# Seventeen products of zeros on TensorE, and a new order of issue on all engines

## The chip, the cores and the metric

The kernel runs on one core of a Trainium2 chip. The metric is device microseconds (us) of one execution, the median of three runs. TensorE (PE in the profile) does the matrix products, VectorE (DVE), ScalarE (ACT) and GpSimd (POOL) the rest, and SyncE (SP) issues nearly all transfers. Each engine works through its own instruction stream in order.

## The reference, cut to what matters

Attention over 4 batches of 8 heads (576 rows of 64 numbers), mixed with a memory term, feeds a gated feed-forward layer:

```python
scores = scale * np.matmul(q, k.transpose(0, 1, 3, 2))
scores = np.where(causal, -1000000000.0, scores)
a = softmax(scores)                      # a /= a.sum(-1) + 1e-09
local = np.matmul(a, v)
mem_out = einsum(phi(q), M_prev) / (einsum(phi(q), z_prev) + 1e-06)
x = g * mem_out + (1 - g) * local        # 2304 rows of 512
xn = x / rms * rms_g
out = (silu(xn @ w_gate) * (xn @ w_val)) @ w_out   # 512 -> 1536 -> 512
```

The three weight matrices arrive as 64-bit floats and are turned into 32-bit ones on the chip.

## The kernel before, in words

The 2304 rows are cut into 18 blocks of 128 rows. Blocks 0 to 3 are the first 128 rows of each batch; their attention is done in 32-bit floats, with TensorE transposes (`transposed`, L524) of k, q, phi(q) and the softmax weights S. The other blocks use pairs of 16-bit numbers. Two blocks make a chunk of 256 rows, and the feed-forward layer runs over nine chunks: `m_proj` (L1037 for chunk 0 in 32 bits, L1044 for the others) makes gate and value, `m_act` (L1061 to L1065) the activation, `m_down` (L1110, L1118 to L1120) the product with w_out.

Ahead of the first product of chunk 0 (`gv`, L1037) stand these steps, for blocks 0 and 1: `transposed` with its copies on ScalarE (L526) or VectorE (L528); the scores (`u_scores`, PE L590, then DVE L607 with the mask and the row maximum); the exponentials (`u_exp`, ACT L656, one for each of the 8 heads of a block); the transposes of S; the products with v (`pv32`, PE L790); their division (`evac32`, DVE L806) and addition to the memory term (POOL L808); the sum of squares (`x_norm`, ACT L384, then POOL L862 and L865); and `x_float`, which multiplies by a diagonal matrix (DVE L876, PE L879) and writes `xT` (DVE L880). The memory term is `mem32` (PE L767 and L771). Beside it the weights are converted: two ScalarE instructions (L955, L956) and one of VectorE (L960) for each piece of 128x512, whose transfer SyncE issues at L922. `over_partitions` (L252, L256) takes a maximum over the 128 partitions by a product with the identity; the first such product is for `zz`, the array of z_prev, whose sum of squares ScalarE makes (L384). `gram` (L272) sums products that bound the scale of k and v.

All engines' orders of issue are written out: the table `ISSUE` holds for PE, Activation, DVE, Pool and SP a string of letters, one letter for a kind of work (`T` a transpose, `s` a gram product, `Z` a maximum over partitions, `S` scores, `E` exponentials, `U` weight conversion, `G` a projection, `D` a down product, and so on), a count behind it, and `~n` to take the n-th of that kind that is left. `keep` marks the functions with their letters, and `issue_in_order` chains each engine's instructions in the table's order. Instructions still wait for their data by semaphores.

Of the kernel before, what the change touches and what calls it, by code (L numbers as in the profile page):

```python
# [62 lines left out]


ISSUE = {
    "PE": (
        "T4s4T4ZT8ZSS~1S~2S~3S4T8u4SS~1S~2S~3T4S4u4Th4T3u2~4s2T2u2~4h4sT6u3h4ush4R4s2~4ss2~3s3R4ZG2G4~6G10Zss2~3ss2~2s2T8"
        "s8T4G4G3~4G5S8ss3~3G4T4u6s2s~1sT4G4ug14g~2gT2ug16T2G2Z2G4~2Z2hs2s3~2G~2G5h3s6s3~1s4s2~2ss~1sT4s4~1ss4~4s4Tu2G3T3"
        "G5h2s4hg16u2hZ2SS~1S~2S~3g2g16~14g12Tg2S4T3u3g3G4ug13Z2G4DhD~1TZ2h2DD~1hT3G8h4D2G5D2G11D2G4G~4DG4DG11D2G12D~1D3"
        "D~1G11D~2DS2S2~6GDS12G12S2M5G6DMM6~2S8M2GM2S6G17SG12ZG12DS7G16S8G8P18GP6G12S8G33S8P9G24MP3DD~2G2M5D~2D3GP12M2S"  # L70
        "G11S~5DD3~2D5M2D3D~3DG4D~2S10G~8DG8S6M3P7D~1G2S2DP5SG9P12M3G10DD~2DD2~1DP2G2~2GPS~3S3D~3P2S2G3~1GP7DG10S3D~2DD~1"
        "DP2DD~2S4P10G4D2~2D2M3G12~5S2G8~5SMG4M~4S3M4GDD2~2D3M7G3D~3D2D2~1DD~3DS~2GS2P18S5DD~1D2P9DP9D2~2D3SG36S3G12D2S"
        "D3~1G4P2SDPG8S6P6G12M3S3PMPDD2~2D2S3~3DMS2~3S2PSP6G12P9MS~1G12P9S5~1DG12M2~2MSD2~2MG10SD3S~5GSD3S~4P3G8~1M2P2"
        "S2~4GS~4S4M2PD3G4D2~3D2G8SGG2~3M2P8GS5G9PG10P4GD~1DD~3G4S~1P3G2SPD~3D3P5G5D~1P4G5PG7PDS3P2DS4G4~5D~1S2G4S4GP7"
        "D2~1DSP2S6~1P6SG6DD~2D2G2P3DSG12P9S8~1D2~1G2SP9G10DD~1M~8G6G~6G7M9G10S3G8D~1D2G~4S~5GS~5MGS~5S5G6~2MD~3S5G2MG5D"
        "D~2P2G7MP10DGDMGSP11GS~7S5MDPGSG9~1PG4S6~1SD2D~1D2S~1PG2D~1P2SDS4G10DD3~1P17G6S~3SGP3G3G~14PDGG4~13SD2~3SGP3"
        "G6~12S2G~12G11PGP3M6D~3G3S~5P13GP3M2S4G8PDGPS8D2P10G11S2DD2~2DD~1DP12G3~12GSS3~5G5D~3G~6D~3D2MS4S~1G~6D~1DG~6S2"
        "G5~6G6D~3GP3S~3G4P7S2G3D~3PSG2~5G5MDD~2G10D~5SM2G6~12PS~6P5S6G4~12G9D2M2G2~3S6P2GG~2G2S4~1P4MGPMS3~1G7P12S~1D5S"
        "G3DD2~2D3G12P12G12S20DD~2DD~1DG21D~1GP3S20DG3~2P8G2PD2~2YP12G4M16S20P8G5D~2G3DP16G2~9G3DG6S20G11D~3D5GDD~2G4D3"
        "G18M14S20P12M2G12P18S15S~1S4P23D2D2~2G7D5D~1DPS20P36DG17P30S15S4~1SDG12D2~3D2D~1DG21SG3D2D~1G4S7G14~8SG3~8G8D3"  # L80
        "S6~7D~3DD~2DD~1S6S2~1G10SG9DG12S3DP120D2~2DD~1S2DG13M8G3~11DG6M8G4DP2S3D~1GPD3D~3D2D2~1DG42P9G4P12G10P12D2~3D4G"
        "P12G7SG5S~5D2D2~1G24S5D4D2~1SD2S4G9M2M2~6M2G3G~12G2M5~4G2M3G6S6MS6D2~3D2D~1DG11S6DD2~2DD~1DMG14S4G10S2G2D~3G2"
        "G12~10S3G6~10S6~3P12G10DD2~2SDP6G6D2~4PDS2P7G12S3DPGS2P8DS3GDG5DS8G5YG4PG6P9D5G2P2MSPGPG11S8~7DG9MP5M2S7P9GM4D~3"
        "D2D~1G2S8GS3D2SP9D3S3~4G8G12~3S~4G3D3M4S4P12G6P11G~6SG10~6DD2~2DS2S4~1G~6S2~1D~1S~1M3PSDGP8G~5G5SMG11D2D2~1DG6D"
        "G4P5G14DD~2DD2~1DG12P~11P4P4~7G12D2D2~1P7~7DP7G12DSP5G3DG9D~2DP2S4~7S7GP5S4P24D3S4G11S4D~3D2D~1MG12~12MG3SG~9G3"
        "M7~6M2S6G2~6SG11M4DG4DMD2~3D4D~3D2D2~1DP8S4S6~2P4S2G12G12~12G12S2P4D2D3~1S4P8G14P5SG6P7G5S4GSM6DG3S4MDG~7G3P12D"
        "G6~4SD~1G5~4MG7~4D2~1DG3S~1GDD~2DP6GS2D~1S3M6P2SGD~1DMG3MG12PS5P4G9S~1DGD2~2SGD~2G2~1P4GD~5D2G2PD5P9S4G26D~3S"
        "D2~3G6P5S4D2G3DP4~4S4GS3P4G5S5P2G7~3SP2G5~3G3D~3G8PD~3D2S~7P7GPGPDP3S5G2DG11DD~2P15S2G6~13GG3~12M4S3MM~3SM~3"
        "G3~12G2M3G8MD~2G~2GS~3MGS~3D3D~3S2P4S2PMG5DPD~2DD~1SDG3MG2S4G12~1G8SMD~3S~7P2MG5DD~2D2S3~7S6S2~1G2P4S3G5D~1P4G5P"
        "G12S2DD2~2DG11P7G13PS3PS3D~1DD~3DD~2D2P10G12P6~12DD3~3G12S20GP12D3G23P6D2P12M14S20G7G2~17G4M2S15S4~1SP6GD2P3"  # L90
        "G2~12D~2G9D2P3S20PG~3PDD~1P4G3P6S20D2~1G7DG12D3~3D3G24S20D~3D2D~1D2P60S16M16S4G36P30S20P30D2D3~1DG24D~3D5G23D8"
        "P120D~1G7~13G13D~1DG10D~1G7DG24DD~1D11D~1DG43D2G3DG~2G21G4~4D5G12D2G9G3~3D4G3D2D~1G7D~1D3G14DD~1D3G12G3~12G31D"
        "D~2DD~1D2G8~2G2DD~2DD~1D2G4D2D3~1G6~12DG12D5G30DG36D~3D5G8D~3D3G16D2D~3D7D3~1DD3~3D3"
    ),
    "Activation": (
        "fI~1TITfTU2TEE2~1ET2IU2E2E~1E2E2~1EE~1E~2E2NU~4UNtU3U4~3U3U~2fAtoAU2~2T3UU~8U~1U~7oU2~3AU3E2~1EfATU3TEUU2~4U2E~2"
        "U2~2EU2E~1EAU2ATxU2xU~2AU3xU2ExEE~1EU3cxNExUXU2xAEE~1EU2U2~2c2U2xU2AxU~1UNxU2XfxckAcqxAU~1Uv~1vkc3qrAxU2x2kcAFxc"
# [18 lines left out]
        "ALV3S2LA4S2LS2LS2A2V3LS2AMLAM2SASALS2LMA2MSXLSV3A2LMA2V3A2XA28O"  # L116
# [1357 lines left out]
```

## Time and profile before

| | us |
|---|---|
| median of three runs | 599.7 (598.3, 599.7, 605.78) |
| the profiled execution, its own time | 599.91 |
| its span, first to last instruction | 597.7 |
| TensorE busy | 579.4 (97%) |
| VectorE, ScalarE, GpSimd busy | 437.9, 394.8, 134.7 |

The profiled execution is 2.2 us longer than its span and 0.2 us longer than the median. The page's mean granted clock of TensorE is 0.997. A matmul's recorded duration holds its latency, so that groups in a row are read by the time from start to start, not by the mean of one.

### The profile page before, as it was taken

Reading aid. Unit: us, or ns where it says so; the run is one execution under the profiler, and the core shown is the slowest. Engines: PE = TensorE matmul, PEld = TensorE weight load, DVE = VectorE, ACT = ScalarE, POOL = GpSimd, SP = SyncE. Lnnn points to the kernel's source line nnn. Section 1 sums busy time; section 2 is a strip of 40 time slices with the busy share of each in tenths; the row PEclk is TensorE's granted clock in tenths of the full one; section 3 lists DMA queues with packets and bytes.
Section 4 is the critical chain, followed back from the end, with each engine's and each line's share of the span. In section 5 each row is a group of like instructions: output and inputs, shape, how many; then the busy total and the mean of one; then the engine's idle time right before and its main releaser. Section 6 shows DMA issues by size and latency. Waiting matters only on the chain.

```text
span 597.7 us, 15764 instructions
## 1 busy us (share of the span) xinstructions
PE 579.4 (97%) x6114; PEld 456.7 (76%) x6114; DVE 437.9 (73%) x1271; ACT 394.8 (66%) x856; POOL 134.7 (23%) x221
## 2 busy tenths in 40 slices
...
PEclk9899999999999999999999999999999999999999
...
GB/s 241 357 321 267 313 158 160 129 166 189 166 112 180 125 168 141 145 166 159 77 148 186 125 143 171 114 135 167 110 157 107 82 125 107 90 64 19 36 1 36
DMA packets 183787, 87.57 MB, mean 146 GB/s; under 512 B 165792, under 2 KB 165792, under 8 KB 183712
## 3 DMA queue, kind: packets, MB, share of 16 engines
...
q14 instruction: 27, 0.22, 0.1%
...
## 4 chain that ended last, share of the span: by engine, by line
PE 64%; DVE 15%; ACT 9%; DMA 7%; issue 3%; POOL 1%; SPq 1%; ACTq 0%; DVEq 0%
PE gv L1044 32%; PE out L1119 5%; PE out L1118 5%; PE out L1120 5%; PE sc L601 3%; DVE S L607 3%; DMA PT<-P 2%; PE gv L1037 2%; DVE P L683 2%; ACT junk L384 2%; DMA kv<-in_qkv_dram 1%; PE sc L624 1%; PE loc L714 1%; DMA wo<-in_moe_w_val_dram 1%; PE loc L715 1%
## 5 line engine op out<-in xcount | busy, mean ns | idle before, releaser
L1044 PE MATMUL gv<-xT,wgv 128*128 128x256 f16 x2304 | 295.6, 273 | 2.8 <-DVE th L1065 2.7
L1044 PEld LDWEIGHTS <-wgv 128*128 128x128 f16 x2304 | 217.0, 98 | 44.8 <-issue 5.4
L1083 POOL TENSOR_TENSOR h<-th,h 128x256 f16<-128x256 f32 x88 | 64.7, 738 | 261.8 <-ACT h L1082 238.5
L683 DVE SCALAR_TENSOR_TENSOR P<-S,P 128x512 f16<-128x512 f32 (+2 forms) x96 | 67.5, 703 | 24.2 <-ACT P L183 24.1
L1061 ACT ACTIVATE th<-gv,wt 128x256 f32<-128x256 f32 x96 | 44.9, 467 | 57.7 <-PE gv L1044 53.9
L1062 DVE SCALAR_TENSOR_TENSOR th<-th,gv 128x256 f32<-128x256 f32 x96 | 39.8, 415 | 57.0 <-ACT th L1061 56.6
L664 ACT ACTIVATE S<-S,nm 128x256 f32<-128x256 f32 (+3 forms) x112 | 69.6, 637 | 17.3 <-DVE nm L607 14.6
L183 ACT ACTIVATE P<-S 128x512 f16<-128x512 f32 (+2 forms) x96 | 57.6, 604 | 14.6 <-DMA PT<-P 13.7
L607 DVE CUSTOM_DVE_ANT_0 S<-sc,mask,qsc 128x256 f32<-128x256 f32 (+2 forms) x96 | 57.3, 610 | 11.4 <-PE sc L601 10.5
L1119 PE MATMUL out<-wo,h 128*128 128x512 f16 x176 | 63.0, 379 | 0.0
L1082 ACT CAST h<-th 128x256 f16<-128x256 f32 x88 | 34.7, 396 | 42.5 <-PE out L1120 32.2
L601 PE MATMUL sc<-kT,qT 128*128 128x128 f16 x576 | 61.0, 219 | 1.4 <-DVE nm L607 1.1
L1118 PE MATMUL out<-wo,h 128*128 128x512 f16 x176 | 62.1, 379 | 0.0
L1120 PE MATMUL out<-wo,h 128*128 128x512 f16 x176 | 61.4, 379 | 0.0
L601 PEld LDWEIGHTS <-qT 128*128 128x128 f16 x576 | 41.9, 98 | 12.2 <-issue 3.4
L1065 DVE SCALAR_TENSOR_TENSOR th<-th,wt,gv 128x256 f32<-128x256 f32 x96 | 45.8, 478 | 2.5
L1037 PE MATMUL gv<-xT,wgv 128*128 128x256 f32 x192 | 44.4, 381 | 0.6 <-DVE xT L880 0.6
L1037 PEld LDWEIGHTS gv<-xT,wgv 128*128 128x128 f32 x192 | 35.5, 190 | 6.9 <-issue 1.6
L715 PE MATMUL loc<-v,PT 128*128 128x64 f16 x288 | 39.3, 194 | 0.0
L716 PE MATMUL loc<-v,PT 128*128 128x65 f16 x288 | 39.2, 192 | 0.0
L714 PE MATMUL loc<-v,PT 128*128 128x65 f16 x288 | 39.1, 193 | 0.0
L851 POOL TENSOR_TENSOR t<-t,t 128x256 f32<-128x256 f32 x28 | 24.5, 880 | 51.8 <-DVE t L848 42.8
...
## 6 DMA issues: line engine op xcount, KB each, us to landing
...
```

The lines of the kernel that those rows point to most:

```text
L183: got = fn(*p, **k)
L601: nc.tensor.matmul(t[:, g * w + j * P : g * w + (j + 1) * P], qT[n][:, t2, h, :], kT[blk_of[(b, j)]][:, h, :], start=(t2 == 0), stop=(t2 = ...
L607: nc.vector.tensor_tensor_reduce(out=s[:, g * w : (g + 1) * w], in0=t[:, g * w : (g + 1) * w], in1=mask[:, m0 : m0 + w], scale=qsc[n][:, 5 ...
L664: nc.scalar.activation(v_, v_, AF.Exp, bias=nm[:, g : g + 1], scale=-1.0)
L683: m = nc.vector.scalar_tensor_tensor(out=p16[:, w : 2 * w], in0=s[:, :w], scalar=PSCALE, in1=p16[:, :w], op0=ALU.mult, op1=ALU.subtract)
L1037: nc.tensor.matmul(o, wgv[:, 1 + p, o0 : o0 + P], xT[0][:, cc, at], start=(cc == 0), stop=(cc == NC - 1))
L1044: nc.tensor.matmul(o, lhs, xT[c][:, rhs, :], start=(cnt == 0), stop=(cnt == 3 * NC - 1))
L1065: nc.vector.scalar_tensor_tensor(out=th, in0=th, scalar=sc_h, in1=gvp[F][:, 1, :], op0=ALU.mult, op1=ALU.mult)
L1083: nc.gpsimd.tensor_tensor(h16[:, 1], th, h16[:, 0], ALU.subtract)
L1118: nc.tensor.matmul(o, hh, whi, start=(f == 0), stop=False)
L1119: nc.tensor.matmul(o, hh, wlo, start=False, stop=False)
L1120: nc.tensor.matmul(o, hl, whi, start=False, stop=(f == NF - 1))
```

## The change

A function `fill` issues products of zeros: the weights are 128 columns of `mask`, the moving operand 256 further columns of it (both zero, 16-bit), and the result goes into a corner of a PSUM tile that the next products overwrite or do not read. The table `FILL` says how many are issued at the n-th call. `fill` is called where `over_partitions`, `total`, `gram`, `transposed`, `x_float` and `m_proj` have taken their PSUM tile; 17 are issued in all. The letter `*` places them in the PE order. All five strings of `ISSUE` are new; of their lines one of each side is shown.

```diff
+FILL = {0: 11, 1: 2, 12: 2, 14: 1, 23: 1}
 ISSUE = {
     "PE": (
-        "T4s4T4ZT8ZSS~1S~2S~3S4T8u4SS~1S~2S~3T4S4u4Th4T3u2~4s2T2u2~4h4sT6u3h4ush4R4s2~4ss2~3s3R4ZG2G4~6G10Zss2~3ss2~2s2T8"
+        "*13*~3sT4sT4s2~2T4Z2T8SS~1S~2S~3S4s3SS~1S~2S~3T8u3S4u5h4u~4sT6u3~4T2h4u3T4h4uh4s2~4ss~3s4*3R8ZG4G5~4G7ss2~3ss2~2"
...
+    fills = [0]
+
+    @keep("*")
+    def fill(t):
+        for _ in range(FILL.get(fills[0], 0)):
+            nc.tensor.matmul(t, mask[:, :P], mask[:, P : 3 * P], start=True, stop=True)
+        fills[0] += 1
+
     @keep("Z")
     def over_partitions(src, n):
         t = ps.tile([P, 512], F32, tag="sc", name="allp")
+        fill(t[:, 256:])
...
     def total(src, n):
         t = ps.tile([P, 512], F32, tag="sc", name="allp")
+        fill(t[:, 256:])
...
                     csum["kv", b, j] = ps.tile([P, 512], F32, tag="out", name=f"csum{j}")
+                    fill(csum["kv", b, j][:, 256:])
...
         t = ps.tile([P, NC, P], F32, tag="gv", name="tp")
+        fill(t[:, :2])
...
         t = ps.tile([P, NC, P], F32, tag="sc", name="xtp")
+        fill(t[:, :2])
...
             gvp[F] = ps.tile([P, 2, 2 * P], F32, tag="gv", name=f"gv{F}")
+            fill(gvp[F][:, 0])
```

The lines of the changed kernel are 13 to 17 higher than those of before: L285, L539, L605, L782, L786, L805, L895 and L1054 of it are L272, L524, L590, L767, L771, L790, L879 and L1037.

**The start of TensorE's stream.** The names are the tiles: `kv_98` k and v of block 0, `q_96` its q, `kv_103` k of block 1, `allp` the maximum over partitions, `tp` a transposed tile, `csum` a gram sum. Before:

```order
L524 MATMUL tp<-ident,kv_98 128x128 x4
L272 LDWEIGHTS kv_98
L272 MATMUL csum_621<-kv_98 128x128
...
L524 MATMUL tp<-ident,q_96 128x128 x4
L252 MATMUL allp<-ident,zq 128x128
L524 MATMUL tp<-ident,ph 128x128 x4
L524 MATMUL tp<-ident,kv_103 128x128 x4
L252 MATMUL allp<-ident,ga 128x128
```

Of the change, with 14 products of zeros, of which three rows are shown:

```order
L255 MATMUL allp<-mask 128x256
...
L255 MATMUL tp<-mask 128x256
...
L255 MATMUL csum_637<-mask 128x256
L285 LDWEIGHTS kv_98
L285 MATMUL csum_637<-kv_98 128x128
L539 MATMUL tp<-ident,kv_98 128x128 x4
...
L539 MATMUL tp<-ident,q_96 128x128 x4
...
L539 MATMUL tp<-ident,ph 128x128 x4
L264 MATMUL allp<-ident,zq 128x128
L264 MATMUL allp<-ident,ga 128x128
L539 MATMUL tp<-ident,kv_103 128x128 x4
```

Eleven products of zeros go into the tile of the first maximum, two into that of the first transpose and one into a gram sum, all ahead of the first data; the transposes of phi(q) of block 0 (`ph`) stand ahead of the product for `zq`, no longer behind it.

**ScalarE from the first copy to the last exponential of blocks 0 and 1.** Before:

```order
L526 COPY q_0_155<-tp 128x512
L506 ACTIVATE ph<-q_101 128x512
L526 COPY q_0_155<-tp 128x512
L955 ACTIVATE wgv<-wgv 128x512
L956 ACTIVATE wgv<-wgv 128x512
L526 COPY k_1_172<-tp 128x512
L656 ACTIVATE S,den<-S,nm 128x128 x4
L526 COPY q_1_179<-tp 128x512 x2
L209 ACTIVATE zhl<-zz,zs 128x32
L955 ACTIVATE wgv<-wgv 128x512
L956 ACTIVATE wgv<-wgv 128x512
L656 ACTIVATE S,den<-S,nm 128x128 x12
```

Of the change:

```order
L541 COPY q_0_168<-tp 128x512 x2
L520 ACTIVATE ph<-q_101 128x512
L212 ACTIVATE zhl<-zz,zs 128x32
L541 COPY k_1_185<-tp 128x512
L541 COPY q_1_192<-tp 128x512
L971 ACTIVATE wgv<-wgv 128x512
L671 ACTIVATE S,den<-S,nm 128x128 x8
L972 ACTIVATE wgv<-wgv 128x512
L541 COPY q_1_192<-tp 128x512
L971 ACTIVATE wgv<-wgv 128x512
L972 ACTIVATE wgv<-wgv 128x512
L671 ACTIVATE S,den<-S,nm 128x128 x8
```

The second copy into `q_0` (phi of block 0) stands ahead of the exponential for `q_101`, and the eight exponentials of block 0 stand in one piece, where four stood before.

**TensorE ahead of the first projection, and GpSimd there.** `S` are softmax weights, `mem` and `zn` the memory term, `loc` the products with v, `PT` transposed weights, `xtp` the product with the diagonal, `gv` the projection. TensorE before:

```order
L790 MATMUL loc_340<-kv_98,PT_280 128x64 x4
L272 LDWEIGHTS kv_98
L272 MATMUL csum_626<-kv_98 128x128
L524 MATMUL tp<-ident,S 128x128 x6
L767 MATMUL mem_326<-Mpair,q_1_179 128x128 x3
L790 MATMUL loc_379<-kv_103,PT_298 128x64 x4
L767 MATMUL mem_326<-Mpair,q_1_179 128x128
...
L790 MATMUL loc_379<-kv_103,PT_350 128x64 x4
L879 MATMUL xtp<-diag,t_0_323 128x128 x4
```

Of the change:

```order
L805 MATMUL loc_353<-kv_98,PT_293 128x64 x4
L782 MATMUL mem_339<-Mpair,q_1_192 128x128 x3
L539 MATMUL tp<-ident,S 128x128 x4
L805 MATMUL loc_394<-kv_103,PT_311 128x64 x4
L782 MATMUL mem_339<-Mpair,q_1_192 128x128
L805 MATMUL loc_394<-kv_103,PT_363 128x64 x4
...
L255 MATMUL gv_469<-mask 128x256
L895 MATMUL xtp<-diag,t_0_336 128x128 x4
L895 MATMUL xtp<-diag,t_1_351 128x128 x4
L264 MATMUL allp<-ident,ssm_480 128x128
L1054 MATMUL gv_469<-xT_383,wgv 128x256 x4
```

Between the last transposes of S and the first `loc` of block 1 the three products of the memory term are gone, and both groups of `xtp` stand together, behind the last three products of zeros. GpSimd before, and of the change, behind the second block's root of the mean square (`xs<-xs,mhalf`):

```order
L865 TENSOR_TENSOR xs<-xs,mhalf 128x1
L460 COPY M_1_501<-zhl 128x16
L744 MEMSET Mpair 128x1024
L745 MEMSET zpair 128x16
```

```order
L880 TENSOR_TENSOR xs<-xs,mhalf 128x1
L474 COPY M_0_492<-zhl 128x16
L760 MEMSET zpair 128x16
L763 COPY zpair<-zz 64x8
L759 MEMSET Mpair 128x1024
```

The large MEMSET of `Mpair` stands two small instructions later.

## Rows read from the trace of the kernel before

**Rows 1.** The page, parts 1 and 2: busy time; granted clock in 40 slices.
```profile
PE 579.4 (97%) x6114; PEld 456.7 (76%) x6114; DVE 437.9 (73%) x1271; ACT 394.8 (66%) x856; POOL 134.7 (23%) x221
...
PEclk9899999999999999999999999999999999999999
```

**Rows 2.** Waits of TensorE over the whole span: total us, times, longest.
```profile
PE tp L524 <- DMA kv<-in_qkv_dram: 5.0, 1, 5.0
PE gv L1044 <- DVE th L1065: 2.7, 3, 1.2
PE xtp L879 <- DVE diag L876: 2.6, 2, 1.9
```

**Rows 3.** Busy time by stretch: us, each engine, granted clock, DMA share, GB/s.
```profile
5.00:10.00 5.00, 4.61 (x22) 4.18 (x23) 2.41 (x11) 2.56 (x8) 2.10 (x6) 1.00 0.92 296
...
20.00:22.00 2.00, 2.00 (x15) 2.00 (x15) 1.20 (x6) 0.63 (x4) 0.72 (x1) 0.62 1.05 385
22.00:24.00 2.00, 2.00 (x12) 2.00 (x11) 1.75 (x5) 0.63 (x2) 0.73 (x1) 0.53 1.02 278
...
80.00:100.00 20.00, 20.00 (x111) 15.63 (x111) 19.82 (x76) 18.18 (x43) 5.27 (x7) 1.00 0.60 171
```

**Rows 4.** Timeline from 0 to 52 us: start, us, engine, line, work [idle before].
```profile
0.91 0.27 DVE L276 MEMSET mask<- 128x256 uint32 x1 [0.91 <-PEq L1461]
...
9.44 0.63 ACT L506 ACTIVATE ph<-q 128x512 f32<-128x512 f32 x1 [0.69 <-PE tp L524]
...
24.00 1.21 ACT L955 ACTIVATE wgv<-wgv 128x512 f32<-128x512 f32 x2
...
27.31 0.28 DVE L876 TENSOR_SCALAR diag<-ident,xs 128x128 f32<-128x128 f32 x1
...
29.95 0.98 POOL L744 MEMSET Mpair<- 128x1024 f32 x1
```

**Rows 5.** The chain that ended last, from 0 to 120 us: start, us, what.
```profile
7.38 0.33 ACT junk L384 x2
7.75 0.80 PE allp L252 x2
8.55 0.87 PE tp L524 x4
...
20.43 1.64 PE loc L790 x8
...
22.18 1.28 PE tp L524 x6
23.46 0.94 PE mem L767 x6
24.39 0.85 PE loc L790 x8
25.34 0.44 DVE t L806
25.82 1.12 PE loc L790 x8
...
27.47 0.72 POOL t L808
...
29.90 1.17 DVE diag L876
31.11 1.17 PE xtp L879 x8
32.31 0.70 DVE xT L880
33.05 7.19 PE gv L1037 x32
...
42.73 0.44 PE tp L524 x4
```

**Rows 6.** The chain that ended last, from 120 us to the end.
```profile
427.07 3.93 PE gv L1044 x36
```

105 lines of the change are left out of this document (53 added, 52 removed).

## The prediction, written before the result was known

> **What bounds the kernel now.** Read the page's busy times first. TensorE is busy 579.4 of 597.7 us and no other engine comes near [rows 1], so its idle time, 18.3 us, is the most that a change of order alone could win there, beside time at the low clock. Then read whose waits they are. One, 5.0 us, is the first transfer, which nothing in the change makes faster. The named waits after it are small: 2.7 us ahead of the products of the later chunks (three waits, the longest 1.2 us) and 2.6 us ahead of the diagonal products [rows 2]. The third view is the chain that ended last: the first projection starts at 33.05 us, and 32 products follow without a break [rows 5]. Late in the run 36 products of 256 columns take 3.93 us, 109 ns each [rows 6], which is 256 columns at 2.4 GHz and about 2 ns more: there TensorE is at full rate, and only less work or an earlier start helps.
>
> So the change is decided ahead of 33 us. Two things in the rows say that there is something to win there. The granted clock is 0.62 and 0.53 in the stretches from 20 to 24 us [rows 3], so 1.52 + 1.88 = 3.4 us at the lower level of 1.2 GHz, while TensorE is on the chain. And the clock that the page shows as full from the start was not: four transposes take 0.87 us at 8.55 us and 0.44 us at 42.73 us on the same chain [rows 5]. The low level at the start lasts to about 10 us.
>
> **The change part by part.** The forecast is made against the profiled execution's 599.91 us, 0.2 above the median of 599.7.
>
> *The 14 products of zeros at the start.* They read the mask, whose first write ends at 0.91 + 0.27 = 1.18 us [rows 4]. At the low clock one takes twice 109 ns, so all take 3.05 us and end near 4.3 us, ahead of the first data at 5.0 us [rows 2]. They lie in a wait and cost nothing; if k came with them still running, the cost would be some tenths, and ScalarE would hide it, as it cannot copy k before the sum of squares of z at 7.38 us [rows 5], behind which its copies stand.
>
> *The three late ones* stand ahead of the diagonal products, in the wait of 2.6 us [rows 2]: 3 x 0.109 = 0.33 us at the high clock, 0.65 at the low one, hidden by VectorE's and GpSimd's work. Should that work be done by then, 0.65 us is the price. I take 0.
>
> *The clock at the start.* If the products of zeros lift it before 7.75 us, the first maximum (0.80) and the transposes of phi (0.87) fall to about half: 0.8 us at most, 0 if the clock rises when it did. The change moves the transposes out from behind the maximum anyway, so I take 0.3.
>
> *The clock from 20 to 24 us.* At full clock the chain's TensorE pieces in it would be 3.4 / 2 = 1.7 us shorter; 0 if the same low stretch comes back. What stood before its fall was small products. The change leaves those but spreads them differently, as the exponentials of block 0 now come in one piece. I take 0.9, the middle.
>
> *ScalarE.* It sits idle 0.69 us ahead of the second exponential of q, waiting for those transposes behind the maximum [rows 4]. In the new order it has the copies to do and TensorE is not held by the maximum. I take 0.6, between 0 and 0.69. The conversions before the last exponential are two pieces in both orders, so the eight exponentials of block 1 end that much earlier.
>
> *The memory term on TensorE.* Six of its products take 0.94 us of the chain between the last transposes and the products with v [rows 5]. In the new order three (six in the trace, since a 32-bit product is issued in two halves) stand ahead of the last transposes, where TensorE waits for the exponentials. I take 0.8 of 0.94; 0 if the transposes are not ready until then either.
>
> *GpSimd's large MEMSET.* The second diagonal takes VectorE 1.17 us, the first 0.28, and beside the second GpSimd writes 1024 columns for 0.98 us from 29.95 us [rows 4, 5]. Two instructions now stand ahead of that MEMSET, beside a copy that stood there before, so that 0.28 us of VectorE fit in first. I take 0.85 of 0.89; 0 if VectorE comes late to it.
>
> *Transfers and weights.* SyncE's order puts one piece of the second third of the weights ahead of the last four of the first. The DMA engines are full there (share 1.02 to 1.05, 278 to 385 GB/s [rows 3]), so half a megabyte costs 1.4 to 1.9 us in landing. ScalarE's conversions have that slack, since two waited until 24.00 us behind a sum of squares [rows 4] and projections follow for 7.19 us that need the pieces one by one. I take 0, with 1.9 as the other end.
>
> *The rest of the order.* From 33 us all five orders are new, but the work is the same. The three waits of 2.7 us may go or double; I take 0, and 2.7 either way for the range.
>
> The sum is 0.3 + 0.9 + 0.6 + 0.8 + 0.85 = 3.45 us. The first projection starts near 29.6 us, and as TensorE hardly waits after it, the end moves by the same: 599.91 - 3.45 = 596.46, and 0.2 less as a median, **596.3 us**.
>
> A rule that speaks against the change: the Trainium skill's page "TensorE: Matmul & The Clock Gate", section "Part 4: PE-mode transpose", says that transposes do not count as busy for the clock. By it the products of zeros would be followed by work that holds no clock, and both clock terms, 1.2 us, would go. The trace is against it: the 22 TensorE products between 5 and 10 us [rows 3] are mostly transposes, and the clock was up soon after.
>
> **The rivals.**
>
> *The gain is eaten later* (0.22). Between 80 and 100 us VectorE is busy 19.82 of 20 us and ScalarE 18.18 [rows 3]. If these or the transfers, and not TensorE, set the pace to there, an earlier first projection meets later weights and TensorE waits. Against it: TensorE shows not one break in that stretch, and VectorE's work too would start earlier. All 3.45 us lost, the time is 599.7.
>
> *The zeros do nothing for the clock* (0.17), by its timing or by the rule above. Then only the order pays: 0.6 + 0.8 + 0.85 = 2.25 us, and the time is 597.5.
>
> *Slower: the clock falls in the wait ahead of the projections* (0.15). Before, eight gram products and the first diagonal products cut that wait into pieces of at most 1.9 us [rows 2], and the clock held. Now the gram products come first and both diagonal groups last, so TensorE has only three products of zeros between the last product with v and the diagonal ones. The wait is then VectorE's division, GpSimd's addition, the sum of squares, its root and the diagonal: 0.44 + 0.72 of it stand in the rows [rows 5], and the execution before took 29.90 - 25.82 = 4.1 us from the last product with v to the diagonal, that product's 1.12 included, so about 3 us. If a fall follows, the projections run at the low level where TensorE is the bound: 1.7 us for a stretch as long as that of 20 to 24 us, 3.4 for two. With the clock terms lost as well: 599.7 - 2.25 + 3.4 = 600.9. It decides if TensorE's idle stretch ahead of the diagonal products is much over 1.9 us and the granted clock goes to 0.50 behind it.
>
> **How the numbers follow.** The forecast has 0.46, the rivals 0.22, 0.17 and 0.15. The forecast's own range reaches from every term at its upper end (0.8 + 1.7 + 0.69 + 0.94 + 0.89 = 5.0 us) with 2.7 us of later waits gone, 592.0, to the clock's terms at nothing with 1 us of new waits, 598.5. The range for all is 592.0 to 600.6: its upper end takes in the first rival and most of the third, and leaves out the dearer end of the third and new waits on top of it. Faster by over 2% would be under 587.7, 12 us, twice the sum of all upper ends: 0.02. Slower by over 2% would be over 611.7: 0.02, for a run of new waits that no row shows. Within 2%, about what a measurement of this kernel can tell from no change, 0.96; the three runs before lie 7.5 us apart.
>
> **What would show it.** The first projection's start tells most: 29 to 30.5 us if the forecast holds, near 33 if not. The transposes of phi in 0.44 us instead of 0.87 would show that the zeros lifted the clock; a granted clock of 1.00 from 20 to 24 us that the low stretch is gone. The second diagonal at 0.28 us shows the MEMSET's term. If the first projection is early and the end is not, the first rival holds, and TensorE's waits then stand behind 33 us; a clock of 0.50 in the first projections shows the third. The forecast is wrong as a whole if the span's change differs from the shift of the first projection by more than 2.7 us.

## The result, and the profile after

The changed kernel takes 604.54 us, the median of 22 runs (602.52 to 607.99), and the kernel before 599.9 us in 22 runs beside it (597.74 to 605.78). The ratio is 1.0066, 95% interval 1.0044 to 1.0089: slower by some 4 us, where 3.45 us of gain were forecast, and 8.2 us above the forecast of 596.3. The profiled execution of the change took 605.68 us, with a span of 603.8 us.

The page of the changed kernel, parts 1 and 2, beside [rows 1]:

```profile
PE 583.4 (97%) x6131; PEld 458.6 (76%) x6131; DVE 445.0 (74%) x1271; ACT 395.3 (65%) x856; POOL 133.7 (22%) x221
...
PEclk9979999999999999999999999999999999999999
```

Its list of what TensorE waited for (us in total, times, longest), beside [rows 2]:

```profile
PE xtp L895 <- DVE diag L892: 2.9, 2, 1.9
PE allp L276 <- DVE mx L448: 1.7, 1, 1.7
PE tp L539 <- ACT S L671: 1.6, 1, 1.6
```

Its chain up to the first projections (start, us, what), beside [rows 5]:

```profile
8.48 1.12 PE tp L539 x4
...
24.55 1.12 PE loc L805 x8
25.73 0.31 issue
26.04 0.68 DVE wgv L976
26.72 0.68 DVE diag L892
27.44 1.17 PE xtp L895 x8
28.63 0.69 DVE xT L896
29.33 1.09 DVE diag L892
30.46 2.09 PE xtp L895 x8
32.57 0.70 DVE xT L896
33.32 9.09 PE gv L1054 x32
```

The last product with v comes 1.27 us earlier than before (24.55, not 25.82), but the first projection 0.27 us later (33.32, not 33.05). Between them stand a weight conversion of VectorE ahead of the first diagonal (0.68 us), and a second group of diagonal products, which starts 0.65 us earlier than before (30.46, not 31.11) and takes 2.09 us for 1.17. Then the 32 projections take 9.09 us, not 7.19. Busy time and granted clock by stretch say why (stretch, its length, busy us of PE, PEld, DVE, ACT and POOL, granted clock, DMA share, GB/s):

```profile
26.00:30.00 4.00, 1.60 (x13) 1.12 (x10) 2.75 (x5) 2.67 (x7) 2.82 (x7) 1.00 1.07 296
30.00:34.00 4.00, 3.19 (x12) 2.80 (x13) 1.83 (x4) 4.00 (x8) 0.90 (x3) 0.55 1.05 386
34.00:38.00 4.00, 4.00 (x13) 3.25 (x12) 2.27 (x4) 0.18 (x1) 0.00 (x0) 0.60 0.92 294
```

The trace's record of the granted clock has it at its lower level from 30.40 to 37.23 us, 6.83 us in place of the 3.41 us from 20.48 on before. Ahead of the fall TensorE was busy 1.60 of 4 us. The same stretches before:

```profile
26.00:30.00 4.00, 2.54 (x24) 2.22 (x24) 2.02 (x7) 1.75 (x5) 2.38 (x7) 1.00 1.05 309
30.00:34.00 4.00, 2.33 (x14) 2.06 (x15) 2.75 (x4) 4.00 (x8) 2.07 (x7) 1.00 1.04 390
34.00:38.00 4.00, 4.00 (x20) 3.51 (x19) 3.76 (x11) 2.40 (x5) 0.00 (x0) 1.00 0.56 181
```

The second place is from 80 to 140 us. First the changed kernel, then the one before, in the same columns:

```profile
40.00:80.00 40.00, 40.00 (x338) 35.96 (x337) 32.23 (x118) 33.54 (x73) 0.88 (x4) 1.00 0.73 251
80.00:140.00 60.00, 56.23 (x336) 40.95 (x334) 53.20 (x166) 52.45 (x121) 11.34 (x18) 1.00 0.60 154
140.00:170.00 30.00, 29.20 (x320) 22.92 (x319) 29.90 (x84) 25.34 (x54) 10.66 (x17) 1.00 0.84 160
```

```profile
40.00:80.00 40.00, 39.74 (x347) 35.88 (x346) 32.92 (x118) 33.26 (x78) 2.27 (x5) 1.00 0.78 284
80.00:140.00 60.00, 59.55 (x367) 43.46 (x367) 56.06 (x176) 55.16 (x123) 13.21 (x20) 1.00 0.68 158
140.00:170.00 30.00, 29.63 (x331) 23.06 (x330) 29.34 (x86) 25.29 (x52) 10.62 (x15) 1.00 0.82 164
```

TensorE is idle 3.77 us from 80 to 140 us, and was 0.45. The same 60 us hold 31 matmul records fewer, and VectorE and ScalarE are each busy some 2.8 us less: they too wait.

**A measure for all runs.** Each run, not only the profiled one, records its span and the mean granted clock. Span times one minus the clock is called *clock loss* here; what is left of the span is the *remainder*. Both are rough. TensorE was not always busy at the low level: over the runs of the kernel before, the span rises 0.6 us for each us of clock loss, so that a kernel with much clock loss shows too small a remainder. And the low level ahead of the first rise is not in it, since the record begins with that rise: the page shows 1.00 from 5 to 10 us [rows 3], where four transposes took 0.87 us and not 0.44. The table has means over the runs with one standard error, and TensorE's busy time from 80 to 140 us in the one profiled execution. Eleven runs that lie more than 1.5% above the fastest of their kernel are left out, e6's profiled execution among them.

| kernel (runs) | span | clock loss | remainder | PE 80-140 |
|---|---|---|---|---|
| before (137) | 598.9 | 3.2 ± 0.2 | 595.7 ± 0.2 | 59.55 |
| after (22) | 602.8 | 4.1 ± 0.3 | 598.7 ± 0.2 | 56.23 |
| e1 changed order, no zeros (8) | 602.6 | 5.2 ± 0.7 | 597.4 ± 0.5 | 57.88 |
| e2 old order, 17 zeros (12) | 599.2 | 3.4 ± 0.6 | 595.8 ± 0.6 | 59.77 |
| e3 new to 33 us, old behind (12) | 601.2 | 5.6 ± 0.8 | 595.5 ± 0.5 | 59.30 |
| e16 new to 80, old behind (12) | 601.0 | 5.0 ± 0.5 | 596.0 ± 0.6 | 59.23 |
| e4 old to 33, new behind (6) | 603.3 | 3.4 ± 1.0 | 599.8 ± 0.9 | 57.16 |
| e9 old to 80, new behind (12) | 603.4 | 3.3 ± 0.7 | 600.1 ± 0.5 | 56.17 |
| e8 old to 170, new behind (12) | 597.1 | 2.7 ± 0.6 | 594.3 ± 0.5 | 59.86 |
| e12 as e8, 28 zeros in the waits (11) | 597.0 | 2.5 ± 0.9 | 594.5 ± 0.3 | 59.83 |
| e15 old order, 28 zeros in the waits (12) | 597.7 | 1.5 ± 0.6 | 596.2 ± 0.3 | 59.34 |
| e10 changed order, 30 zeros in the waits (12) | 599.0 | 3.0 ± 0.3 | 596.0 ± 0.2 | 58.17 |
| e14 as e10, conversions behind (12) | 599.0 | 2.7 ± 0.7 | 596.3 ± 0.3 | 58.77 |
| e13 changed, conversions behind (12) | 602.7 | 4.6 ± 0.9 | 598.0 ± 0.3 | 57.18 |
| e11 changed, conversions early (12) | 602.9 | 5.1 ± 0.7 | 597.8 ± 0.5 | 56.91 |
| e17 changed, w_out early (10) | 604.8 | 6.3 ± 0.8 | 598.5 ± 0.6 | 58.18 |
| e18 as e10, w_out early (12) | 602.0 | 4.6 ± 0.7 | 597.4 ± 0.3 | 57.87 |
| e5 changed, old transfers (6) | 637.3 | 15.1 ± 1.4 | 622.3 ± 1.2 | 56.83 |
| e6 before, GpSimd without reads (11) | 596.3 | 3.2 ± 0.8 | 593.1 ± 0.5 | 59.72 |
| e7 changed, the same (11) | 599.2 | 4.9 ± 0.8 | 594.3 ± 0.6 | 57.40 |

So of the 3.9 us of span, 0.9 ± 0.4 is clock loss and 3.0 ± 0.3 remainder; with 0.6 us of span for each us of clock loss, the shares are 0.5 and 3.3.

### The profile page after: what moved, and what is told of

Its sections match the earlier page's. It is cut to its first block, busy times and chain, and to the rows that moved or that the text cites. A ratio compares the mean times of both kernels' runs of the same rounds, so it can differ in the third digit from the quotient of the medians.

```text
span 603.8 us, 15802 instructions
## 1 busy us (share of the span) xinstructions
PE 583.4 (97%) x6131; PEld 458.6 (76%) x6131; DVE 445.0 (74%) x1271; ACT 395.3 (65%) x856; POOL 133.7 (22%) x221
## 4 chain that ended last, share of the span: by engine, by line
PE 72%; DVE 13%; ACT 5%; DMA 5%; issue 2%; SPq 1%; ACTq 0%; POOL 0%; DVEq 0%
PE gv L1061 33%; PE out L1135 6%; PE out L1137 6%; PE out L1136 6%; PE gv L1054 4%; PE sc L616 4%; DVE S L622 2%; ACT junk L397 2%; DMA wo<-in_moe_w_out_dram 1%; DVE row L215 1%; PE sc L639 1%; PE tp L539 1%; DMA kv<-in_qkv_dram 1%; PE csum L285 1%; PE loc L730 1%
## 5 line engine op out<-in xcount | busy, mean ns | idle before, releaser
L698 DVE SCALAR_TENSOR_TENSOR P<-S,P 128x512 f16<-128x512 f32 (+2 forms) x96 | 65.4, 683 | 13.0 <-ACT P L186 12.9
L1136 PE MATMUL out<-wo,h 128*128 128x512 f16 x176 | 64.1, 379 | 0.0
L1135 PE MATMUL out<-wo,h 128*128 128x512 f16 x176 | 63.1, 379 | 0.1
L1137 PE MATMUL out<-wo,h 128*128 128x512 f16 x176 | 61.7, 379 | 0.0
L1054 PE MATMUL gv<-xT,wgv 128*128 128x256 f32 x192 | 46.8, 393 | 0.4 <-DVE xT L896 0.4
L1054 PEld LDWEIGHTS gv<-xT,wgv 128*128 128x128 f32 x192 | 37.0, 198 | 8.3 <-issue 2.9
```

The costliest lines, as they stand in the source:

```text
L698: m = nc.vector.scalar_tensor_tensor(out=p16[:, w : 2 * w], in0=s[:, :w], scalar=PSCALE, in1=p16[:, :w], op0=ALU.mult, op1=ALU.subtract)
L1054: nc.tensor.matmul(o, wgv[:, 1 + p, o0 : o0 + P], xT[0][:, cc, at], start=(cc == 0), stop=(cc == NC - 1))
L1135: nc.tensor.matmul(o, hh, whi, start=(f == 0), stop=False)
L1136: nc.tensor.matmul(o, hh, wlo, start=False, stop=False)
L1137: nc.tensor.matmul(o, hl, whi, start=False, stop=(f == NF - 1))
```

## The experiments

**Order or zeros (e1, e2).** The edit of e1 in the changed kernel, and of e2 in the kernel before, to which `fill` is added:

```diff
-FILL = {0: 11, 1: 2, 12: 2, 14: 1, 23: 1}
+FILL = {}
-        "*13*~3sT4sT4s2~2T4Z2T8SS~1S~2S~3S4s3SS~1S~2S~3T8u3S4u5h4u~4sT6u3~4T2h4u3T4h4uh4s2~4ss~3s4*3R8ZG4G5~4G7ss2~3ss2~2"
+        "sT4sT4s2~2T4Z2T8SS~1S~2S~3S4s3SS~1S~2S~3T8u3S4u5h4u~4sT6u3~4T2h4u3T4h4uh4s2~4ss~3s4R8ZG4G5~4G7ss2~3ss2~2sT4sZs8"
```
```diff
-        "T4s4T4ZT8ZSS~1S~2S~3S4T8u4SS~1S~2S~3T4S4u4Th4T3u2~4s2T2u2~4h4sT6u3h4ush4R4s2~4ss2~3s3R4ZG2G4~6G10Zss2~3ss2~2s2T8"
+        "*13*~3T4s4T4ZT8ZSS~1S~2S~3S4T8u4SS~1S~2S~3T4S4u4Th4T3u2~4s2T2u2~4h4sT6u3h4ush4*3R4s2~4ss2~3s3R4ZG2G4~6G10Zss2~3s"
```

> The changed kernel's order on all engines, without the 17 products of zeros. In the changed kernel's profile the clock was low from 30.40 to 37.23 us, over the last diagonal products and the first projections (9.09 us for 32, against 7.19), and TensorE's waits behind 33 us were some 4 us longer than before. Theory A, the order alone loses the time: as slow as the change, 603 to 605 us. Theory B, the products of zeros lose it, because the clock rises early and then falls in the projections: 600 to 601 us, with no low clock in the first projections.

> The order of the kernel before on all engines, with the 17 products of zeros added: 14 at the start, 3 ahead of the first diagonal products. Theory A (the order loses): 599 to 600 us, as before. Theory B (the zeros lose): 602 to 604 us, with a granted clock of 0.50 behind 28 us.

Measured: e1 604.27 us, ratio to before 1.0064 [1.0028, 1.0100]; e2 601.09, ratio 1.0011 [0.998, 1.0042]. The order alone makes the loss, and the 17 zeros show no effect in the old order. In e2's profiled execution they did lift the clock, at 3.91 us, and it fell again at 7.33 and came back at 17.57:

```profile
4.00:6.00 2.00, 1.14 (x12) 0.93 (x11) 0.00 (x0) 0.51 (x2) 0.00 (x0) 1.00 0.97 339
6.00:8.00 2.00, 0.39 (x4) 0.15 (x2) 1.19 (x3) 0.71 (x4) 0.26 (x2) 0.83 0.87 233
8.00:12.00 4.00, 4.00 (x18) 3.77 (x19) 2.62 (x12) 3.32 (x8) 1.84 (x5) 0.50 0.93 342
```

**Where the order costs (e3, e4, e8, e9, e16).** All five strings are cut at one time: what had started by then in the one kernel's trace keeps its order, and the rest follows in the other's. SyncE's string of the changed kernel as e16 and e9 have it, first of their lines:

```diff
-        "bl2blm2Wl~1Wm~1mW~4lW~1W~5WlW~1WbWd3l~1d3~1a4W~1W~2W~3dW~1lbW2dW2W~1W2l~1la2Wa2W~1WbWbB~1B2B~1B~2B3XB3Xk2Bl~1rlk"
+        "bl2blm2Wl~1Wm~1mW~4lW~1W~5WlW~1WbWd3l~1d3~1a4W~1W~2W~3dW~1lbW2dW2W~1W2l~1la2Wa2W~1WbWbB~1B2B~3B5XB2XkBlkr3kFbrl2"
```
```diff
-        "bl2blm2Wl~1Wm~1mW~4lW~1W~5WlW~1WbWd3l~1d3~1a4W~1W~2W~3dW~1lbW2dW2W~1W2l~1la2Wa2W~1WbWbB~1B2B~1B~2B3XB3Xk2Bl~1rlk"
+        "lbl~1bm~1mW2l~1m~1mll~1WdW2W~1ld2W~1Wd3~1dW~1ba2W~1a2WW~3bW~1l~1lW2W~1lWW~1dW3~1WB~2la2ba2WbB~5WB2B~1B3XB3Xk2B"
```

> Every engine issues what the changed kernel had issued up to its first projection (33.2 us in its profile), zeros included, in the changed order, and all the rest in the order of before. If the head loses the time (the clock that falls ahead of the projections, 2.8 us on the path): 602 to 603 us. If the rest of the order loses it (the 4 us of later waits): 599 to 600 us. If each has its part: the sum with the next run is the change's loss of about 4.5 us.

> The reverse: up to the first projection (33.0 us in the profile of before) the order of before without zeros, and all the rest in the changed order. If the rest loses the time: 603 to 605 us, with waits of TensorE of 1 us and more between 85 and 160 us and between 350 and 390 us. If the head loses it: 599 to 600 us.

> Every engine's order is that of before for all that had been issued up to 170 us, without zeros, and the changed one behind it. If the loss of the new order lies between the projections' start and 170 us, where TensorE's waits are 5.7 us against 2.1: the time of before, 599 to 601 us. If it lies behind 170 us: 603 to 605.

> The old order up to 80 us, without zeros, and the new order behind. Theory C (the loss is made between 33 and 80 us: conversions of the expert weights stand behind the first activations of the projections on ScalarE and VectorE, so their buffers come free late, the transfers into them stop for some 5 us, and TensorE pays for it later): the wait of SyncE for a weight buffer stays near 5 us as before, and the time is 597 to 600, as with the old order up to 170 us (598.25). Rival D (the new order of VectorE between 80 and 170 us costs TensorE its waits by itself): 602.5 to 605, as with the old order up to 33 us (605.41). Between 600.5 and 602: both take part.

> The changed order with its zeros up to 80 us, the old order behind. If the loss is made behind 80 us: span less clock loss 595.5 to 596.5, as the old order, and a time of 600 to 602 by its clock. If it is made between 33 and 80 us (transfers stopped near 50 us): 597.5 or more, and 603 to 605.

Measured: e3 602.23 us (1.0043 [1.0007, 1.0079]), e4 605.41 (1.0085 [1.0055, 1.0114]), e8 598.25 (0.9954 [0.9915, 0.9994]), e9 605.56 (1.0065 [1.0032, 1.0098]), e16 602.64 (1.0023 [0.9995, 1.005]). In the table two costs part. With the new order in front (e1, e3, e16) the clock loss is 5.0 to 5.6 us, and with the old order behind 33 or 80 us (e3, e16) the remainder is that of before. With the new order behind 33 or 80 us (e4, e9) the clock loss is that of before and the remainder 4 us more. With it behind 170 us alone (e8) the remainder is 1.4 ± 0.5 us lower than before. e8 and e9 differ only in the order from 80 to 170 us, and by 5.8 ± 0.7 us of remainder: this stretch costs more than the 3.0 us of the whole change, which has the gain behind it in it. Theory C, by which the loss is made between 33 and 80 us, falls. The parts do not add up: in span e3 lies 2.2 us and e4 4.3 us above before, 6.5 together, where the whole change has 3.9; so a cut from one order to the other has an effect of its own, and these sizes are rough. The times of e4, e9 and e16 lie up to 0.6 us above the ranges that fit best, and e8's lies 0.8 below. The windows of e16 and of e9:

```profile
80.00:140.00 60.00, 59.23 (x360) 43.07 (x359) 55.67 (x173) 54.35 (x123) 13.27 (x20) 1.00 0.67 155
```
```profile
80.00:140.00 60.00, 56.17 (x319) 40.11 (x318) 51.13 (x160) 51.60 (x115) 12.30 (x17) 0.97 0.59 145
```

Every kernel with the old order in this stretch keeps TensorE busy 59.2 us or more of the 60, every one with the new order 56.2 to 58.8.

**The clock ahead of the projections (e10, e15, e12).** More zeros, placed ahead of the first group of diagonal products, between the two and behind (10, 16, 4 in the changed order; 8, 16, 4 in the old):

```diff
-FILL = {0: 11, 1: 2, 12: 2, 14: 1, 23: 1}
+FILL = {0: 11, 1: 2, 12: 2, 14: 28, 23: 1}
-        "*13*~3sT4sT4s2~2T4Z2T8SS~1S~2S~3S4s3SS~1S~2S~3T8u3S4u5h4u~4sT6u3~4T2h4u3T4h4uh4s2~4ss~3s4*3R8ZG4G5~4G7ss2~3ss2~2"
+        "*13*~30sT4sT4s2~2T4Z2T8SS~1S~2S~3S4s3SS~1S~2S~3T8u3S4u5h4u~4sT6u3~4T2h4u3T4h4uh4s2~4ss~3s4*10R4*16R4*4ZG4G5~4G7s"
```
```diff
+FILL = {12: 2, 14: 26}
-        "T4s4T4ZT8ZSS~1S~2S~3S4T8u4SS~1S~2S~3T4S4u4Th4T3u2~4s2T2u2~4h4sT6u3h4ush4R4s2~4ss2~3s3R4ZG2G4~6G10Zss2~3ss2~2s2T8"
+        "T4s4T4ZT8ZSS~1S~2S~3S4T8u4SS~1S~2S~3T4S4u4Th4T3u2~4s2T2u2~4h4sT6u3h4ush4*8R4s2~4ss2~3s3*16R4*4ZG2G4~6G10Zss2~3s"
```

> The changed kernel with 30 late zero products in place of 3: 10 ahead of the first diagonal product, 16 between the two groups and 4 behind the second. Theory K (a good part of the loss is the clock that falls ahead of the gate and value projections): no low stretch between 28 and 37 us, the second group of eight in 1.16 us, 32 projections in 7.2 us, first projection at 32.5 or earlier, and a time of 601.5 to 603. Theory C (transfers decide): the first projection comes a microsecond earlier, and the time stays at 603.5 to 605, since the transfers wait for conversions that start no earlier than the first activation. If the clock falls in spite of the zeros, nothing is decided and the time is 604 to 605.

> The old order throughout with 28 zero products (8, 16, 4) around the two groups of diagonal products. If zeros in these waits keep the clock high: span times one minus the granted clock falls from 3.46 to 2 or less, and with it and the earlier start of the projections the time is 596 to 599. If they only work together with the new order: 600 to 602, as the old order.

> The old order up to 170 us with 28 zero products around the two groups of diagonal products (8, 16, 4), the new order behind. Beside 598.25 for the same without zeros: theory K says 596.5 to 597.5 if the clock is kept high from the first diagonal product to the projections; if the transfers set the pace of this stretch, 598 to 599.

Measured: e10 600.85 us (0.9986 [0.9958, 1.0014]), e15 599.58 (0.9974 [0.9944, 1.0003]), e12 597.61 (0.9941 [0.9904, 0.9978]). In e10's profiled execution the clock stays up:

```profile
26.00:30.00 4.00, 3.77 (x34) 3.23 (x32) 2.75 (x5) 2.73 (x7) 2.88 (x7) 1.00 1.08 273
30.00:34.00 4.00, 3.76 (x25) 3.07 (x23) 2.75 (x5) 4.00 (x8) 0.83 (x3) 1.00 1.06 320
34.00:38.00 4.00, 4.00 (x20) 3.54 (x19) 1.29 (x3) 0.20 (x1) 0.00 (x0) 1.00 1.03 371
...
80.00:140.00 60.00, 58.17 (x354) 42.31 (x353) 54.06 (x176) 53.05 (x118) 12.13 (x20) 1.00 0.67 163
```

```profile
30.39 1.17 PE xtp L895 x8
...
32.34 7.17 PE gv L1054 x32
```

Theory K holds: 30 zeros bring back all of the loss within the interval, more than the 1.5 to 3 us expected. In all five profiled executions with 28 or 30 such zeros (e10, e12, e14, e15, e18) the 32 projections take 7.17 us on the timeline; of the other fifteen only that of the kernel before has this, and fourteen take 7.50 to 10.23. And the zeros do more than keep a clock: the remainder falls too, by 2.8 us, and TensorE is busy 58.17 us from 80 to 140 us, though the order there is the changed one. So the price of the order behind 80 us is not fixed by that order alone; what else makes it is open. A late, slow first group of projections may make the waits behind 80 us longer, but that is not shown: e1's began at 33.97 us and took 7.84, with 57.88 us busy there, nearly e10's, and e9's began at 32.16 us and took 7.51, and it keeps the loss. In the old order (e15) the clock loss halves, as expected, but the time falls between the two ranges, and its gain is at the edge of its interval. e12, which beats both kernels, joins the old order up to 170 us, the new one behind and these zeros; e8 without zeros is close to it, so that the zeros show no clear effect there.

**Which wait behind 80 us (e11, e13, e14, e17, e18).** In the changed kernel SyncE waits 12.3 us for a buffer of weights at 40 us, and no transfer moves a byte from 49 to 54 us; before, the longest such wait was 5.3. It waits for a conversion of VectorE, queued behind the first activations, as its partners on ScalarE are. e11 moves them ahead (ScalarE, then VectorE):

```diff
 L520 ACTIVATE ph<-q_209 128x512
+L972 ACTIVATE wo<-wo 128x512
+L971 ACTIVATE wgv<-wo 128x512
+L972 ACTIVATE wo<-wo 128x512
+L971 ACTIVATE wgv<-wo 128x512
 L1078 ACTIVATE h32e<-gv_469 128x256
```
```diff
 L976 SCALAR_TENSOR_TENSOR wgv<-wgv 128x512 x5
+L976 SCALAR_TENSOR_TENSOR wgv<-wgv,wo 128x512 x2
 L1079 SCALAR_TENSOR_TENSOR h32e<-h32e,gv_469 128x256
```

> The changed kernel with six conversions on ScalarE (four into its idle 7 us ahead of the first activation, two behind the first rounding step) and three on VectorE moved earlier. Theory C: SyncE's wait for a weight buffer falls from 12.3 us to under 5, the stop of the transfers near 50 us is gone, the waits of TensorE between 80 and 170 us shrink from 5.7 us to under 3, and the time is 599.5 to 602. Rivals K (clock) and D (order of VectorE at 80 to 170 us): 603.5 to 606.

Measured: 604.3 us, 1.0048 [1.002, 1.0076]. The longest wait of that stretch went from 12.3 to 4.8 us, and the time hardly followed (remainder 0.9 ± 0.5 less); the transfers now stop from 60 to 63 us. The waits of SyncE from 33 to 60 us, in the changed kernel and in e11:

```profile
SPq L938 <- DVE wgv L976: 15.7, 3, 12.3
```
```profile
SPq L938 <- DVE wgv L976: 10.8, 4, 4.8
```

At 88 us a single wait can be followed. ScalarE of the changed kernel, and TensorE in the last row:

```profile
86.25 0.39 ACT L671 ACTIVATE S<-S,nm 128x128 f32<-128x128 f32 x1
...
88.59 0.66 ACT L971 ACTIVATE wo<-wo 128x512 f32<-128x512 f32 x1 [1.86 <-DMA wo<-in_moe_w_out_dram]
89.16 0.64 ACT L972 ACTIVATE wo<-wo 128x512 int32<-128x512 uint16 x1
89.70 0.39 ACT L671 ACTIVATE S<-S,nm 128x128 f32<-128x128 f32 x1
...
90.62 0.33 PE L539 MATMUL tp<-ident,S 128*128 128x128 f32 x1 [1.59 <-ACT S L671]
```

A conversion whose transfer is late stands at the head of ScalarE's queue, the exponential behind it is what TensorE's transpose needs, and TensorE stands for 1.59 us. e13 puts two such pairs behind the work that TensorE waits for (first of the two places), e14 does so in e10:

```diff
-L671 ACTIVATE S,den<-S,nm 128x128
+L671 ACTIVATE S,den<-S,nm 128x128 x4
 L971 ACTIVATE wo<-wo 128x512
-L972 ACTIVATE wo<-wo 128x512
-L671 ACTIVATE S,den<-S,nm 128x128 x3
-L972 ACTIVATE wo<-wo 128x512
+L972 ACTIVATE wo<-wo 128x512 x2
```

> The changed kernel with two pairs of conversions of the last weights moved on ScalarE behind the work that TensorE waits for (the pair at 88.6 us behind three exponentials, the pair at 120.1 us behind the row of k, a weight and the gate's difference; on VectorE one conversion behind one maximum). Theory H (a conversion that waits for a late transfer stands ahead of what TensorE needs): the gaps of 1.75 us at 88.75 and of 1.22 us at 123.78 on TensorE go, and span less clock loss falls from 598.7 to 596 to 597; time 601.5 to 602.5. Rival (these gaps are taken up by slack behind them, and the loss is VectorE's total): 604 to 605, as the changed kernel.

> The same moves in the changed order with 30 late zeros (600.85 without the moves). There the first gap is only 0.33 us, the second 1.24: theory H gives 599 to 600.2; its rival 600.5 to 601.2.

Measured: 603.69 us (1.0048 [1.0015, 1.0082]) and 600.56 (0.9989 [0.9961, 1.0017]). The first gap went, and others took its place; e14's time is its rival's, e13's lies between the two and nearer to its rival's. e13's waits of TensorE from 80 to 140 us:

```profile
PE gv L1061 <- DVE th L1082: 1.7, 1, 1.7
PE gv L1054 <- DVE h32e L1082: 1.1, 1, 1.1
```

e17 and e18 bring the output weights in earlier: a transfer into a free buffer that stood behind a blocked one on SyncE, and the conversions that free two buffers (VectorE shown):

```diff
+L976 SCALAR_TENSOR_TENSOR wo<-wo 128x512
 L622 ISA S,nm<-sc,mask 128x128
...
+L976 SCALAR_TENSOR_TENSOR wo<-wo 128x512
 L463 COPY tcb_920<-cb_479 64x24
...
-L976 SCALAR_TENSOR_TENSOR wo<-wo 128x512 x2
```

> The changed kernel with the conversions of the first two output weights ahead: on ScalarE one moved from behind four exponentials to ahead of them (81.7 to 79 us), on VectorE two from 81.9 and 83.0 us to around four masked maxima at 78.9; and on SyncE one transfer into a free buffer from 84.1 to 69 us. Theory W (late transfers of the output weights make the loss behind 80 us): the transfer issued at 83.73 goes at 81 or earlier, ScalarE's wait of 1.86 us at 88.59 falls under 0.5, TensorE is busy 58 of the 60 us from 80 to 140 in place of 56.2, span less clock loss 596.5 to 597.5, time 601 to 603. Rival (VectorE's order and GpSimd beside it make the loss): 597.8 to 598.8 and 603.5 to 605, with the gaps moved on as in e13.

> The same moves in the changed order with 30 late zeros (600.85, span less clock loss 595.95). Theory W: 594.5 to 595.5 and a time of 599 to 600. Rival: 596, and 600.5 to 601.5.

Measured: 606.45 us (1.008 [1.0047, 1.0113]) and 604.11 (1.0048 [1.0021, 1.0076]), both slower than without. ScalarE's wait at 88 us is gone, but the four exponentials near 80 us begin 0.74 us later in e17 (80.89, not 80.15), TensorE waited 0.49 us (e18: 1.31) for an exponential at 81 us, and in both profiled executions the clock then fell for 6.83 us. e17, the same columns:

```profile
80.00:82.00 2.00, 1.45 (x11) 0.90 (x10) 1.97 (x12) 2.00 (x8) 0.33 (x1) 1.00 0.06 16
82.00:84.00 2.00, 1.89 (x7) 1.30 (x7) 2.00 (x7) 1.54 (x6) 1.53 (x2) 0.71 0.93 301
84.00:86.00 2.00, 2.00 (x11) 1.91 (x9) 1.27 (x9) 1.65 (x5) 0.70 (x2) 0.50 0.51 207
86.00:90.00 4.00, 4.00 (x22) 2.97 (x22) 2.28 (x10) 3.45 (x12) 0.05 (x1) 0.54 0.03 6
```

The moves took one wait away and made another, so they do not show theory W, and they do not exclude it.

**Two that decided less (e5; e6 and e7).** e5 gives SyncE the old string in the changed kernel:

```diff
-        "bl2blm2Wl~1Wm~1mW~4lW~1W~5WlW~1WbWd3l~1d3~1a4W~1W~2W~3dW~1lbW2dW2W~1W2l~1la2Wa2W~1WbWbB~1B2B~1B~2B3XB3Xk2Bl~1rlk"
+        "lbl~1bm~1mW2l~1m~1mll~1WdW2W~1ld2W~1Wd3~1dW~1ba2W~1a2WW~3bW~1l~1lW2W~1lWW~1dW3~1WB~2la2ba2WbB~5WB7XB2XkBlkr3kFbr"
```

> The changed kernel with SyncE's order of transfers of before; all else is the change, zeros included. In the change ScalarE stood still for pieces of w_out near 118 us and VectorE waited behind it. Theory T (the new order of transfers makes the loss): 600 to 601 us, and TensorE's waits from 80 to 170 us fall from 5.7 us to 2. Theory P (VectorE's instructions are stretched beside GpSimd's): 604 to 605 us, with VectorE still busy some 444 us.

Measured: 639.42 us, 1.0619 [1.0564, 1.0675]. The transfers' order has to fit the other four, so this tells nothing of what the new one costs by itself.

e6 (kernel before) and e7 (changed) take the large reads of GpSimd out, since VectorE is busy 7 us more in the changed kernel. They leave out the low halves of what GpSimd splits and most of one addition:

```diff
-        nc.gpsimd.tensor_tensor(dst_lo, src, dst_hi, ALU.subtract)
+        nc.gpsimd.memset(dst_lo, 0.0)
...
-            t1s[n][:, four(n, g4), :], t1s[n][:, four(n, g4), :], t2[:, four(n, g4), :], ALU.add,
+            t1s[n][:, 4 * g4, :8], t1s[n][:, 4 * g4, :8], t2[:, 4 * g4, :8], ALU.add,
...
-        nc.gpsimd.tensor_tensor(h16[:, 1], th, h16[:, 0], ALU.subtract)
+        nc.gpsimd.memset(h16[:, 1], 0.0)
```

> The kernel before with GpSimd's work between the projections left small: in place of the 96 subtractions of the activation's low half and the 5 of the weights' it writes zeros, and of the 28 additions of memory and local term it does 8 columns, so that part of the result is left out. Theory P: VectorE's stretched instructions go (some 438 us busy falls by 8 to 10), and the time falls by less than 2 us, to 598 to 600. Theory T: the same time as before, 600.

> The changed kernel with the same GpSimd work left out (zeros for the low halves, 8 columns of the additions). Theory P: VectorE's 445 us busy fall to the same 428 to 430 as in the run of the old order, and the difference of the two orders falls from 4 us to under 2: 599 to 601 us. Theory T: the difference stays near 4 us: 603 to 604.

Measured: 597.79 us (0.9961 [0.993, 0.9993]) and 601.24 (0.9991 [0.9948, 1.0034]). The medians differ by 3.45 us, as theory T has it; but of the remainder the difference is 1.2 ± 0.7 us in place of 3.0, of VectorE's busy time 3.2 us (426.8 against 430.0) in place of 7.1, and TensorE loses 2.3 us between 80 and 140 us (59.72 against 57.40) in place of 3.3. So VectorE's instructions that are stretched beside GpSimd's can be a part of the gap and are not shown to be all of it; the two runs don't decide between P and T.

## Why the prediction was wrong

Two steps failed: the gain of 3.45 us ahead of the first projection, which did not come, and the nothing that was put in for the order behind it. By the prediction's own sign it is wrong as a whole: the profiled spans differ by 6.1 us, the first projections by 0.27.

**The rest of the order.** The step is "*The rest of the order.* From 33 us all five orders are new, but the work is the same ... I take 0, and 2.7 either way". Its size is the remainder's 3.0 ± 0.3 us, at the bound that I gave it; e3, e16, e8 and e9 put the loss between 80 and 170 us, and the profiled windows put most of it between 80 and 140. The same work in another order was not the same time. TensorE, VectorE and ScalarE were each busy over 91% of the time from 80 to 140 us before, and VectorE 19.82 of 20 us from 80 to 100 us [rows 3]. I read that as a rival's ground and as no cost, since TensorE showed no break. That the missing slack is the reason is argued, not shown: e6 and e7, with less for VectorE to do, point that way. What stays open is which pieces of the order make the loss, and why 30 zeros ahead of the projections take 2.8 us of it away (e10). Single waits were moved (e11, e13, e17), the gaps moved on, and at most 0.9 us of the remainder came back.

**The head** was to bring the first projection to 29.6 us; it came at 33.32, and in no profiled execution with the new head ahead of 32.34. Term by term:

- *14 zeros at the start, 0*: right, they end at 4.4 us, ahead of the first data. These came at 5.94 us and not at 5.0, since SyncE's new order has a transfer of q ahead of k and v; in e2, with the zeros and the old transfers, they came at 5.09. That delay had no term.
- *Clock at the start, 0.3*: nothing. It rose at 9.92 us (10.24 before), and the transposes of phi took 1.12 us on the chain (0.87 before), not 0.44. In e11 and e17, whose start is the same, the clock rose at 4.53 and 4.34 us, but it fell again at 7.94 and 7.75, ahead of these transposes, and the scores began at 11.77 and 11.61 us, later than the changed kernel's 11.06.
- *Clock from 20 to 24 us, 0.9; ScalarE, 0.6; memory term, 0.8*: the low stretch there is gone in the profiled execution, and with the other two the last product with v came 1.27 us earlier, where 2.6 with the first clock term were forecast. The runs don't part the three. In e13's execution, with the same head, a low stretch came back from 19.20 to 26.02 us.
- *MEMSET, 0.85*: the "0 if VectorE comes late to it" came true. VectorE wrote xT at 28.63 us for 0.69 us, and the second diagonal took 1.09 us again. Not foreseen was the conversion of 0.68 us that the order puts ahead of the first, nor that the first would take 0.68 us for 0.28.
- *Transfers, 0*: but for the first data, not tested by themselves (e5).

**The third rival** ("the clock falls in the wait ahead of the projections", 0.15) is what the profiled execution shows in the head. The size was near: 6.83 us at the low level, priced at 3.4, cost 0.92 us in the second diagonal group and 1.90 in the projections. Its condition did not hold: no idle stretch was longer than 1.9 us, as before. Its reason, the eight gram products that no longer stand between the two groups (28.63 us before), fits TensorE's busy time there, 1.60 of 4 us and 2.54 before, but it is not shown. With the old order and the gram products in place the clock fell at that point too, in the profiled executions of e2, e4, e6 and e8 at 34.63, 35.54, 33.60 and 33.36 us, and their 32 projections took 8.81, 7.96, 10.23 and 7.97 us. e2, in the columns of above:

```profile
34.00:40.00 6.00, 5.44 (x19) 4.44 (x18) 5.41 (x13) 4.01 (x8) 0.00 (x0) 0.72 0.45 157
```

So the one execution of the kernel before on which the forecast rests, with full clock there, was luck. Over all runs the new head does lose more clock, 4.1 to 5.6 us in seven kernels (after, e1, e3, e7, e11, e13, e16) against 2.7 to 3.4 in six with the old head (before, e2, e4, e6, e8, e9). By that rival's own sum the time was 600.9, but that sum has 2.25 us of gain in it, and the second diagonal group started 0.65 us earlier.

**The other two rivals.** The zeros did not help, as the second had it (0.17), but the order did not pay either. The first (0.22) needs an early first projection, which did not come; its ground, VectorE nearly full from 80 to 100 us, lies in the stretch where the rest of the order lost.

**The rule on transposes** (the Trainium skill's page "TensorE: Matmul & The Clock Gate", section "Part 4: PE-mode transpose") I set aside because the clock rose behind a stretch of transposes. It spoke for dropping both clock terms; the first came to nothing, and the second is not parted from its neighbours. e2 agrees with it in so far as the clock fell at 7.33 us, soon after transposes; but TensorE was busy only 0.39 of the 2 us around that time, so no run here parts the two.
